# Float32 products in two column blocks, spread test loads and a first table of higher rank in a one-core attention and mixture-of-experts kernel

## The chip, the core and the metric

The kernel runs on one core of a Trainium2 chip. The metric is the device time of one launch in microseconds (us). Three runs of the kernel before gave 805.13, 809.86 and 812.39 us, so the median is 809.86 us. Engines are named as in the profile: PE is TensorE (matrix products), DVE is VectorE, ACT is ScalarE, POOL is GpSimd, and SP is the queue that issues most DMAs.

## The reference

Three stages follow one another: a linear attention with decay, a feed-forward product with a leaky relu, and a top-1 mixture of eight experts.

```python
def _attn_ref(q, k, v, alpha):           # each (4, 8, 768, 48), float32
    for t in range(S):
        state = alpha[:, :, t, :, None] * state + np.einsum('bhd,bhe->bhde', k[:, :, t], v[:, :, t])
        y[:, :, t] = np.einsum('bhd,bhde->bhe', q[:, :, t], state)

def _moe_ref(x, w_in, w_out):            # x (3072, 384), w_in (384, 2048), w_out (2048, 384)
    h = x @ w_in
    g = np.maximum(0.01 * h, h)
    return g @ w_out

def _moe2_ref(x, w_gate, w1, w2):        # w_gate (384, 8), w1 (8, 384, 1024), w2 (8, 1024, 384)
    logits = x @ w_gate
    expert_idx = np.argmax(logits, axis=1)
    # gate_w: softmax probability of the chosen expert
    for e in range(E):
        h = np.maximum(x[mask] @ w1[e], 0.0)
        out[mask] = gate_w[mask, None] * (h @ w2[e])
```

The weights w_in and w_out reach the kernel as float64 bit patterns, pairs of 32-bit words.

## The kernel before, in words

The 3072 tokens are cut into eight units (u) of 384 tokens, each of three chunks (c) of 128. Large products are made as three float16 products of high and low parts. In outline, the work of one unit is this.

- Attention: decays (`decays`, line 556 and on, DVE and ACT) are scanned, keys and queries are scaled by them (`scaled`, lines 594 and 596), keys are transposed (`keys`, line 619), scores are made (`chunk`, line 690, 48 rows by 128 columns) and masked (lines 692 and 694). The values of a chunk are scores times values (line 727) plus queries times the running state (line 715). Units 0 and 1 do line 727 in float32, the others in float16. The state itself is updated in `running` (line 651, weights of 64 columns, two heads in the two halves of the output's partitions). Chunk 0 of units 0, 2, 4 and 6 has no running state, so line 715 runs for 20 of the 24 chunks.
- After a chunk's values, DVE takes the largest magnitude (line 734) and makes a power of two of it (`pow2`, lines 518 to 523), ACT scales (line 738), PE transposes (lines 746 and 748), ACT and DVE write the two halves of `xT`.
- Feed-forward (`moe1`): the first product of a unit is 16 column blocks of 9 PE instructions (line 796), each followed by the leaky relu (`leaky`, lines 773 to 780), the second product is 144 PE instructions (line 805). `finish` (from line 851) splits its rows, and `route` (from line 879) chooses experts and scatters the rows of the unit to DRAM on POOL's queue (line 931).
- Weights first: while unit 0 runs, `w_in_piece` makes float32 and then a high and a low float16 part of each of 12 pieces of w_in from the float64 bits. The low part is made by two products on PE (lines 426 and 427) for pieces 0 to 2 and by DVE (line 422) for pieces 3 to 11. `w_out_piece` does the like for 16 pieces of w_out, and `logit_weights` multiplies each by w_gate (line 459 transposes, line 469 three float32 products of 8 columns).
- The float64 test: `low_load` reads all weights a second time in 56 pieces (SP, line 512, tile `ck`, three buffers), and DVE takes the smallest magnitude of the low words of each (line 514). It may run once the last w_out piece is done and unit 2 has had its first products.
- Experts: after unit 6 is routed, `tile_table` computes for 14 token tiles which expert and which rows they hold; `tile_gathers` gathers a tile's rows (POOL, line 1134, with a DVE copy of its list, line 1131), and `turn` transposes it (line 1147, six PE instructions). The last unit's rows are routed, and 14 further tiles listed, inside the expert loop (`last_tiles`). The expert loop (`experts`) makes 112 rounds, of 18 instructions at line 1245 and 6 at line 1271; each forces as many turns as it needs, and may take one turn more if its gather was issued at least `AHEAD1` = 4 rounds earlier by `state["gathered"]`.

The order on every engine up to the expert loop is written out at build time by a small planner, class `Loom`. Each piece of work is a generator that yields operations `O(engine, planned us, ...)`; `need` names events that must have happened, `take` and `free` count buffers, `post` makes an event, and each chain has a rank (the second argument of `loom.add`, the lowest first). The planner takes whichever operation can start first by its own clocks, and among those within 0.25 us of it the one of lowest rank. An event that a DMA posts counts as happened 2 us (in planned time before 130) or 4 us after its issue; an operation that merely follows a DMA in the same generator is not given that time. `keep_warm` fills planned gaps of PE with products that nobody reads (line 371). The engines then run their lists in that order, each waiting for its real inputs. In the expert loop the order is that of the code.

## Time and profile before

| | before |
|---|---|
| median of the runs | 809.86 us |
| the profiled execution, its own time | 808.41 us |
| its span, first to last instruction | 806.6 us |
| PE busy | 767.6 us, 95% |
| DVE busy | 639.6 us, 79% |
| ACT busy | 494.1 us, 61% |
| POOL busy | 370.1 us, 46% |

Times in the trace count from the first instruction. The first product of unit 0 (line 796) starts at 46.8, of unit 1 at 140.4, of unit 2 at 209.6, of unit 3 at 277.8, of unit 4 at 351.3, of unit 7 at 507.5; the last second product (line 805) of unit 7 ends at 557.2, and the expert loop fills the rest. A stage is read from one such start to the next. A float32 product may show two records. The granted clock of PE in a window is given as a share of 2.4 GHz: 1.00 is that level all the time, and a lower figure is a mean with stretches at 1.2 GHz.

### The profile page before, as it was taken

What the parts mean: (1) busy time and instruction counts of PE and PEld (TensorE: products, weight loads), DVE (VectorE), ACT (ScalarE), POOL (GpSimd) and SP (SyncE); (2) the same over time, 40 slices, a digit from 0 to 9 for tenths busy, and PEclk for the clock granted to TensorE, in tenths of its full rate; (3) what the DMA queues carried; (4) which work ended last, traced back from release to release, by engine and by line L of the source; (5) the groups of instructions that cost most, each with busy time, mean ns of one, the idle gap of its engine ahead of it and who ended that gap; (6) DMA issues with size and microseconds to landing.
All of it is one profiled execution on the core that took longest, in us unless ns stands there. A gap on an engine that the chain in (4) does not pass through costs nothing.

```text
span 806.6 us, 19210 instructions
## 1 busy us (share of the span) xinstructions
PE 767.6 (95%) x6991; PEld 541.3 (67%) x6991; DVE 639.6 (79%) x1450; ACT 494.1 (61%) x1137; POOL 370.1 (46%) x375
## 2 busy tenths in 40 slices
PE   7969999999997998999999999998999999999994
PEld 3836777667665565666756565666788888778883
DVE  7898999999787899975745485668668888999674
ACT  3647566799994268765454374643476566566673
POOL 6016313484373256245234061344531588776553
PEclk9899999999999999999999999999999999999998
DMA  9762454223417776200100323127354244332221
GB/s 261 247 170 79 121 157 118 61 71 90 99 44 209 214 194 186 61 1 1 51 1 3 127 70 98 43 86 210 95 150 140 90 120 137 100 119 61 93 82 69
DMA packets 44421, 87.23 MB, mean 108 GB/s; under 512 B 4797, under 2 KB 29427, under 8 KB 44320
## 3 DMA queue, kind: packets, MB, share of 16 engines
q1 hardware_dynamic: 39104, 70.89, 30.7%
q0 software_dynamic: 5216, 15.02, 5.6%
q8 instruction: 60, 0.98, 0.5%
q14 instruction: 41, 0.34, 0.1%
HBM read 76.42 MB, written 10.25 MB: 107 GB/s over the span
## 4 chain that ended last, share of the span: by engine, by line
PE 52%; DVE 9%; DMA 5%; issue 4%; POOL 3%; ACT 2%; POOLq 0%; ACTq 0%; DVEq 0%
PE a L1245 13%; PE m L1271 13%; PE m L796 13%; PE m L805 9%; DMA ck<-in_moe_w_in 2%; DMA ck<-in_moe_w_out 2%; DVE g_w L514 1%; DMA acc<-x_rows,offj 1%; POOL acc L1134 1%; PE a L1147 1%; POOL gh L780 1%; DVE Sd L640 1%; DVE gf L775 1%; PE a L690 1%; DVE Ft L556 1%
## 5 line engine op out<-in xcount | busy, mean ns | idle before, releaser
L796 PE MATMUL m<-xT,wih 128*128 128x384 f16 x1152 | 197.4, 331 | 7.9 <-DVE gf L775 7.8
L805 PE MATMUL m<-woh,gh 128*128 128x392 f16 x1152 | 202.9, 330 | 0.8 <-DVE gf L775 0.8
L780 POOL TENSOR_TENSOR gh<-gf,gh 128x384 f16<-128x384 f32 x118 | 113.8, 973 | 173.9 <-ACT gh L778 173.6
L796 PEld LDWEIGHTS <-wih 128*128 128x128 f16 x1152 | 113.3, 99 | 83.5 <-issue 13.1
L805 PEld LDWEIGHTS <-gh 128*128 128x128 f16 x1152 | 111.2, 98 | 73.7 <-issue 2.3
L1245 PEld LDWEIGHTS <-st 128*128 128x128 f16 x2016 | 123.5, 99 | 14.6 <-DVE st L1178 0.7
L1245 PE MATMUL a<-XT,st 128*128 128x128 f16 x2016 | 132.8, 221 | 0.0
L1271 PE MATMUL m<-W,hs 128*128 x672 | 128.2, 328 | 0.3 <-issue 0.3
L775 DVE SCALAR_TENSOR_TENSOR gf<-m,gf 128x384 f32<-128x384 f32 x128 | 69.9, 553 | 48.7 <-ACT gf L773 47.6
L1178 DVE COPY st<-W 128x1536 f16 x112 | 86.6, 773 | 22.3 <-PE a L1245 12.2
L773 ACT ACTIVATE gf<-m 128x384 f32<-128x384 f32 x128 | 62.2, 488 | 47.7 <-PE m L796 45.8
L1253 ACT ACTIVATE hs<-a 128x256 f16<-128x256 f32 x112 | 42.5, 379 | 65.1 <-PE a L1245 54.9
L1271 PEld LDWEIGHTS <-hs 128*128 128x128 f16 x672 | 61.6, 99 | 30.2 <-issue 1.2
L778 ACT CAST gh<-gf 128x384 f16<-128x384 f32 x128 | 64.2, 507 | 16.0 <-DVE gf L775 15.6
L1070 POOL TENSOR_TENSOR W<-wr,W 128x768 f16<-128x768 f32 x32 | 57.9, 1809 | 14.2 <-ACT W L1069 14.2
L1257 DVE SCALAR_TENSOR_TENSOR hs<-a,hs 128x256 f16<-128x256 f32 x112 | 46.5, 415 | 12.0 <-ACT junk L1289 7.5
L1286 DVE SCALAR_TENSOR_TENSOR acc<-m,acc 128x384 f32<-128x384 f32 x84 | 51.0, 607 | 1.7 <-issue 0.4
L1134 POOL DMA_INDIRECT acc<-x_rows,offj x28 | 29.4, 1049 | 39.5 <-DVE offj L1131 33.1
L1043 POOL TENSOR_SCALAR wr<-wr 128x768 f32<-128x768 f32 x32 | 32.7, 1024 | 26.9 <-DMA wr<-in_moe_w 26.9
L1292 POOL DMA_INDIRECT out<-acc x28 | 29.1, 1038 | 28.4 <-DVE acc L1286 21.6
L352 ACT ACTIVATE scrap<-W 128x768 bf16<-128x768 f16 x48 | 40.0, 834 | 0.0
L931 POOL DMA_INDIRECT x_rows<-xg,pi x24 | 26.1, 1087 | 21.5 <-DVE xg L925 9.3
(253 smaller groups left out, 1223.7 us busy)
## 6 DMA issues: line engine op xcount, KB each, us to landing
wr<-in_moe_w SPq DMA_DIRECT2D x64, 384.0 KB, 3.1
al<-in_aT SPq DMA_DIRECT2D x16, 390.0 KB, 3.2
raw_in<-in_moe_w_in SPq DMA_DIRECT2D x12, 512.0 KB, 9.9
raw<-in_moe_w_out SPq DMA_DIRECT2D x16, 384.0 KB, 3.9
ck<-in_moe_w_in SPq DMA_DIRECT2D x24, 256.0 KB, 2.8
ck<-in_moe_w_out SPq DMA_DIRECT2D x32, 192.0 KB, 2.4
kn__143<-in_kT SPq DMA_DIRECT2D x16, 288.0 KB, 5.3
qn__146<-in_qT SPq DMA_DIRECT2D x16, 288.0 KB, 9.3
```

The costliest lines, as they stand in the source:

```text
L773: A.activation(gf, ph[:, 0:UT], AF.Copy, scale=0.01 * CG)
L775: V.scalar_tensor_tensor(gf, ph[:, 0:UT], CG, gf, ALU.mult, ALU.max)
L778: A.copy(gh[:, 0], gf)
L780: E_[e].tensor_tensor(out=gh[:, 1], in0=gf, in1=gh[:, 0], op=ALU.subtract)
L796: T.matmul(ph[:, 0:UT], wih[:, a, kk, f * P : (f + 1) * P], xT[:, b, kk, :], start=(n == 0), stop=(n == 8),)
L805: T.matmul(po[:, 0:ROW], g[f][:, a, c * P : (c + 1) * P], woh_[0][:, b, f, :], start=(n == 0), stop=(n == 3 * NF - 1),)
L1070: G.tensor_tensor(out=lo, in0=raw, in1=hi, op=ALU.subtract)
L1178: V.tensor_copy(out=sth[i % 2].rearrange("p a k f -> p a (k f)"), in_=Wp[ph][0][:, :, ds(reg(V, j), 1), :, :].rearrange("p a e k f -> p a ...
L1245: T.matmul(hp[:, f * P : (f + 1) * P], st[:, a, kk, f * P : (f + 1) * P], XT[j][:, b, kk, :], start=(n == 0), stop=(n == 8),)
L1257: V.scalar_tensor_tensor(hs[:, 1].rearrange("p i t -> p (i t)"), hp[:, 0 : 2 * P], 0.0, hs[:, 0].rearrange("p i t -> p (i t)"), ALU.max, A ...
L1271: T.matmul(yp[:, 0:DM], hs[:, a, i, :], W2[:, b, ds(rp, 1), i, :].rearrange("p e f -> p (e f)"), start=(n == 0), stop=(n == 5),)
L1286: V.scalar_tensor_tensor(ac, yp[:, 0:DM], gt, ac, ALU.mult, ALU.add)
```

## The change

Five edits are made.

1. Float32 products whose weights have 128 columns are issued as two products of 64 weight columns, each to its half of the output's partitions: the scores times values of units 0 and 1, the queries times state of all units, and the logit products. The queries times state now come behind the scores times values. The planned durations of these, and of the unchanged line 651, are lowered.
2. The test loads may start when unit 1 has had its first products (before: unit 2). A load needs the landing of the load two before it. The landing is an event with 2 us added, and the DVE operation needs it.
3. Pieces 3 to 5 of w_in have their low part made on PE as well.
4. The first table has rank 0.9 instead of 1.5, so that it comes ahead of the leaky relu's chains, which have 1. GAP, the planned spacing of gathers, is 0.8 instead of 1.2.
5. The gathers that the planner places carry their planned time in rounds after the planner's end of PE, where they had counted as nine rounds before the loop.

```diff
--- before.py
+++ after.py
@@ -51,7 +51,7 @@
 EXPM = 0x7F800000
 RING = 3
 AHEAD1 = 4
-GAP = 1.2
+GAP = 0.8
 F64_TINY = 2.0**15 / 1.125
 F64_LOW = 2.0**-15 * 1.125
 RMAX = 2.0**58
@@ -417,7 +417,7 @@
         hi, lo = (wih[:, a, kk, sl] for a in range(2))
         yield O("A", 0.65)
         A.activation(hi, w32, AF.Copy, scale=SA)
-        if n >= 3:
+        if n >= 6:
             yield O("v", 0.63, free=[("w32", ("i", n))], post=[("wi", n)])
             V.scalar_tensor_tensor(lo, w32, SA, hi, ALU.mult, ALU.subtract)
             return
@@ -463,10 +463,13 @@
             A.activation(wt, pt[:, 0:DM], AF.Copy, scale=SB)
         else:
             V.tensor_scalar(wt, pt[:, 0:DM], SB, None, ALU.mult)
-        yield O("P", 0.67, take=[("a", ("lg", f))], free=[("wt", f)])
+        yield O("P", 0.35, take=[("a", ("lg", f))], free=[("wt", f)])
         pg = pst("a")
         for kk in range(3):
-            T.matmul(pg[:, 0:E], wt[:, kk * P : (kk + 1) * P], wg[:, kk, :], start=(kk == 0), stop=(kk == 2))
+            for m in range(0, P, 64):
+                T.matmul(
+                    pg[m : m + 64, 0:E], wt[:, kk * P + m : kk * P + m + 64], wg[:, kk, :], start=(kk == 0), stop=(kk == 2)
+                )
         yield O("A", 0.4, free=[("a", ("lg", f))])
         A.copy(og[:, f, :], pg[:, 0:E])
         A.copy(woh[:, 0, f, DM:ROW], og[:, f, :])
@@ -500,7 +503,7 @@
 
     def low_load(i):
         n, h = divmod(i, 2)
-        yield O("D", 0.9, need=["lp", ("first", 2)], take=[("ck", i)])
+        yield O("D", 0.9, need=["lp", ("first", 1)] + ([("lo", i - 2)] if i > 1 else []), take=[("ck", i)], post=[("lo", i)], lag=2.0)
         raw = lp[0].tile([P, 256, 2], U32, tag="ck", name="ck", bufs=3)
         w = 256 if n < 12 else DM // 2
         if n < 12:
@@ -510,7 +513,7 @@
         else:
             src = w_out[(n - 12) * P : (n - 11) * P, h * w : (h + 1) * w]
         nc.sync.dma_start(out=raw[:, 0:w].rearrange("p a b -> p (a b)"), in_=src.bitcast(U32))
-        yield O("V", 0.07 + 0.28 * w / 256, free=[("ck", i)], post=[("low", i)])
+        yield O("V", 0.07 + 0.28 * w / 256, need=[("lo", i)], free=[("ck", i)], post=[("low", i)])
         V.tensor_reduce(g_w[:, i : i + 1], raw[:, 0:w, 1].bitcast(F32), AX.X, ALU.min, apply_absolute_value=True)
 
     def pow2(mx, kexp, n, nm):
@@ -642,7 +645,7 @@
                 )
                 loom.add(heads(u, c, Sc), (4 + 2 * u if u else 0.5) - 0.05, now=loom.clock["V"])
             if c in states(u):
-                yield O("P", 0.92, need=[("kn", u, c), ("vt", u)] + ([("vy", u)] if u >= US else []), apart=True,
+                yield O("P", 0.5, need=[("kn", u, c), ("vt", u)] + ([("vy", u)] if u >= US else []), apart=True,
                         take=[("a", ("u", u, c)), ("SU", (u, c))], free=[("kn", (u, c)), ("vt", u)])
                 up = pst("a")
                 vt = r["vt"]
@@ -704,28 +707,34 @@
                 e = yield O("G", 1.17, post=[("shl", u, c, z)], alt=("v", (0.6,), 0.3))
                 E_[e].tensor_tensor(out=sh[:, 1, z], in0=s_[z], in1=sh[:, 0, z], op=ALU.subtract)
             loom.add(scores_range(u, c, s_), 7 + u)
-            yield O("P", 1.45 if old else 0.8, need=Sn + [("vs", u, i) for i in range(c + 1)], take=[YA, ("xh", (u, c)), ("n1", (u, c))],
+            yield O("P", 1.3 if old else 0.7, need=Sn + [("vs", u, i) for i in range(c + 1)], take=[YA, ("xh", (u, c)), ("n1", (u, c))],
                     free=[("sh", (u, c)), ("vs", u)] + Sf, post=[("y", u, c)])
         else:
-            yield O("P", 2.85 if old else 1.95, need=Sn + [("vt", u)], take=[YA, ("xh", (u, c)), ("n1", (u, c))], free=[("sm", (u, c)), ("vt", u)] + Sf, post=[("y", u, c)])
+            yield O("P", 1.65 if old else 1.0, need=Sn + [("vt", u)], take=[YA, ("xh", (u, c)), ("n1", (u, c))], free=[("sm", (u, c)), ("vt", u)] + Sf, post=[("y", u, c)])
         yp = pst("a")
-        n, tot = 0, (3 * H if half else H) + (4 if old else 0)
-        if old:
-            for pr in range(4):
-                T.matmul(
-                    yp[:, pr * 96 : pr * 96 + 96], qt[:, pr, sl], r["Sc", c][:, pr, :],
-                    start=(n == 0), stop=(n == tot - 1), skip_group_check=True,
-                )
-                n += 1
+
+        r64 = [slice(64 * m, 64 * m + 64) for m in range(2)]
         for h in range(H):
             hd = slice(h * D, (h + 1) * D)
             if half:
-                ab = [(sh[:, a, h % 2, h // 2, :], r["vs"][:, b, c, hd]) for a, b in ((0, 0), (0, 1), (1, 0))]
+                for i, (a, b) in enumerate(((0, 0), (0, 1), (1, 0))):
+                    T.matmul(
+                        yp[:, hd], sh[:, a, h % 2, h // 2, :], r["vs"][:, b, c, hd],
+                        start=(h == 0 and i == 0), stop=(not old and h == H - 1 and i == 2), skip_group_check=True,
+                    )
             else:
-                ab = [(s_[h % 2][:, h // 2, :], r["vt"][:, c, hd])]
-            for a, b in ab:
-                T.matmul(yp[:, hd], a, b, start=(n == 0), stop=(n == tot - 1), skip_group_check=True)
-                n += 1
+                for m in r64:
+                    T.matmul(
+                        yp[m, hd], s_[h % 2][:, h // 2, m], r["vt"][:, c, hd],
+                        start=(h == 0), stop=(not old and h == H - 1), skip_group_check=True,
+                    )
+        if old:
+            for pr in range(4):
+                for m in r64:
+                    T.matmul(
+                        yp[m, pr * 96 : pr * 96 + 96], qt[:, pr, c * P + m.start : c * P + m.stop], r["Sc", c][:, pr, :],
+                        start=False, stop=(pr == 3), skip_group_check=True,
+                    )
         yield O("V", 1.0)
         if half:
             mx = g_y[:, 3 * (u - US) + c : 3 * (u - US) + c + 1]
@@ -1165,7 +1174,7 @@
             place_of(j)
             gather(j)
             reg(V, j)
-            state["gathered"].append(state["tile"])
+            state["gathered"].append(state["tile"] if late is not None else loom.clock["G"])
             loom.ev["gap", j] = loom.clock["G"] + GAP, "G"
 
     def tile_turns():
@@ -1219,11 +1228,12 @@
         loom.add(low_load(i), 10 + 0.01 * i)
     loom.add(moe1(), 50)
     loom.add(first_weights(), 20)
-    loom.add(first_table(), 1.5)
+    loom.add(first_table(), 0.9)
     loom.add(firsts, 0.5, True)
     loom.add(turns, 3.5, True)
     loom.add(first_stages(), 3.6)
     loom.run()
+    state["gathered"] = [int((t - loom.clock["P"]) / 2.3) for t in state["gathered"]]
 
 
 
```

The edits move work on all engines. Three places are shown.

The first is on DVE in the middle of the kernel before, from the largest magnitude of unit 4's second chunk (`g_y<-a`) to the rows of unit 2 (`mx<-m`, `n2m`, `L`); `g_w<-ck` is the test of one loaded piece. Before:

```order
L734 TENSOR_REDUCE g_y<-a 128x1
L518 TENSOR_SCALAR n1m<-g_y 128x1
L522 TENSOR_SCALAR n1s<-n1m 128x1
L523 TENSOR_SCALAR n1e<-n1m 128x1
L514 TENSOR_REDUCE g_w<-ck 128x1 x2
L851 TENSOR_REDUCE mx<-m 128x1
L518 TENSOR_SCALAR n2m<-mx 128x1
L522 TENSOR_SCALAR n2s<-n2m 128x1
L523 TENSOR_SCALAR n2e<-n2m 128x1
L853 TENSOR_SCALAR L<-m,n1e 128x8
L854 SCALAR_TENSOR_TENSOR gsc<-n1e,n2e 128x1
L514 TENSOR_REDUCE g_w<-ck 128x1 x3
```

And now, from the same chunk:

```order
L743 TENSOR_REDUCE g_y<-a 128x1
L521 TENSOR_SCALAR n1m<-g_y 128x1
L525 TENSOR_SCALAR n1s<-n1m 128x1
L526 TENSOR_SCALAR n1e<-n1m 128x1
L869 SCALAR_TENSOR_TENSOR xg<-m,n2s,xg 128x384
L566 SCALAR_TENSOR_TENSOR ln,g_fr<-Ft,R 128x780
L517 TENSOR_REDUCE g_w<-ck 128x1
L568 SCALAR_TENSOR_TENSOR R<-ln,R 128x780
L599 SCALAR_TENSOR_TENSOR kt<-kn__143,R 128x12x64
L743 TENSOR_REDUCE g_y<-a 128x1
```

Between the second and the third chunk of unit 4 stood seven tests, and now there is one. The first test stands ahead of unit 3's first chunk now (before: of unit 4's), the last ahead of unit 7's first chunk (before: of unit 5's second).

The second place is on PE, the last rows ahead of the first product of unit 1 (`m<-xT,wih`); `xh` is a chunk's scaled values, `kn` a chunk's keys, `ident` with a number the filler's operand. Before:

```order
L755 MATMUL a<-xT,idn_161 128x384
L619 MATMUL a<-ident,kt 128x128 x4
L746 MATMUL a<-ident,xh 128x128 x3
L651 MATMUL a<-vt,kn 64x48 x8
L755 LDWEIGHTS idn_161
L755 MATMUL a<-xT,idn_161 128x384
L690 MATMUL a<-qt,kt 128x128 x8
L796 LDWEIGHTS wih
L796 MATMUL m<-xT,wih 128x384
```

And now:

```order
L371 LDWEIGHTS ident_65
L371 MATMUL m<-ident_65 128x512
L371 LDWEIGHTS ident_65
L371 MATMUL m<-ident_65 128x512
L764 LDWEIGHTS idn_161
L764 MATMUL a<-xT,idn_161 128x384
L371 LDWEIGHTS ident_65
L371 MATMUL m<-ident_65 128x512
L371 LDWEIGHTS ident_65
L371 MATMUL m<-ident_65 128x512
L805 LDWEIGHTS wih
L805 MATMUL m<-xT,wih 128x384
```

The second products of unit 0 are all done earlier now, and two groups of key transposes, a state update and a group of scores have moved behind the first product of unit 1, so that fillers stand between the last transposes. In all there are 85 filler products (70 before), of which 18 stand between unit 0's last second product and unit 1's first product, where there was none.

The third place is on POOL, around the scatters of the last unit's rows (`x2_rows<-xg`); `acc12` and `acc13` are the last two of the first 14 tiles. Before:

```order
L1134 DMA acc9_5812<-x2_rows,offj_68 128x386
L1134 DMA acc10_5813<-x2_rows,offj_68 128x386
L1134 DMA acc11_5814<-x2_rows,offj_68 128x386
L930 COPY xg_6961<-con_97 128x1
L931 DMA x2_rows<-xg_6961,pi_7465 24577x386
L930 COPY xg_7091<-con_97 128x1
L931 DMA x2_rows<-xg_7091,pi_7465 24577x386
L930 COPY xg_7226<-con_97 128x1
L931 DMA x2_rows<-xg_7226,pi_7465 24577x386
L1134 DMA acc12_5815<-x2_rows,offj_68 128x386
L1134 DMA acc13_5816<-x2_rows,offj_68 128x386
```

And now:

```order
L1143 DMA acc10_6013<-x2_rows,offj_68 128x386
L1143 DMA acc11_6014<-x2_rows,offj_68 128x386
L1143 DMA acc12_6015<-x2_rows,offj_68 128x386
L1143 DMA acc13_6016<-x2_rows,offj_68 128x386
L939 COPY xg_7243<-con_97 128x1
L940 DMA x2_rows<-xg_7243,pi_7719 24577x386
L939 COPY xg_7387<-con_97 128x1
L940 DMA x2_rows<-xg_7387,pi_7719 24577x386
L939 COPY xg_7515<-con_97 128x1
L940 DMA x2_rows<-xg_7515,pi_7719 24577x386
L1143 DMA acc14_7540<-x2_rows,offj_68 128x386
L1143 DMA acc15_7541<-x2_rows,offj_68 128x386
```

The gathers of all first 14 tiles stand ahead of the scatters now. On PE, nine of the turns stand ahead of the first round of the expert loop (before: six), the next comes after round 3 (before: one each after rounds 0, 1 and 4).

On SP, the 56 test loads stood in a nearly closed row with two decay loads and a key load between them; now 17 rows of loads of decays, keys, queries and values stand among them.

## Rows read from the trace of the kernel before

**Rows 1.** Page, busy time by engine: us, share of the span, instructions.

```profile
PE 767.6 (95%) x6991; PEld 541.3 (67%) x6991; DVE 639.6 (79%) x1450; ACT 494.1 (61%) x1137; POOL 370.1 (46%) x375
```

**Rows 2.** Windows by stage: window, length, busy us of PE, PEld, DVE, ACT, POOL; clock.

```profile
46.80:140.40 93.60, 85.50 (x655) 63.09 (x654) 86.72 (x165) 58.43 (x145) 29.26 (x37) 0.96 0.42 122
...
209.60:277.80 68.20, 62.44 (x516) 40.32 (x514) 50.67 (x135) 43.30 (x105) 32.29 (x33) 0.97 0.49 141
277.80:351.30 73.50, 69.33 (x631) 45.81 (x629) 69.56 (x162) 50.38 (x113) 33.07 (x30) 0.98 0.50 138
...
557.20:600.00 42.80, 38.70 (x466) 32.38 (x464) 27.57 (x105) 24.59 (x46) 21.13 (x23) 0.92 0.47 135
```

**Rows 3.** Timeline of PE, 245 to 318 us: start, length, instruction, count, idle before it.

```profile
...
253.44 0.55 PE L748 MATMUL a<-ident,xh 128*128 128x128 f32 x3 [1.95 <-ACT xh L738]
262.36 0.90 PE L748 MATMUL a<-ident,xh 128*128 128x128 f32 x3 [2.42 <-ACT xh L738]
```

**Rows 4.** Source line 514: idle of DVE ahead of it, us and times.

```profile
...
  DMA ck<-in_moe_w_in: 6.9, 11
  DMA ck<-in_moe_w_out: 3.3, 8
```

**Rows 5.** Chain of waits, 238 to 320 us: start, length, what.

```profile
...
243.07 3.80 DMA ck<-in_moe_w_in
246.90 0.43 DVE g_w L514
247.34 2.98 DMA ck<-in_moe_w_in
```

**Rows 6.** Timeline of PE, 505 to 600 us.

```profile
...
562.54 0.82 PE L1147 MATMUL a<-ident,acc 128*128 128x128 f16 x6 [2.20 <-DMA acc<-x_rows,offj]
...
581.11 0.51 PE L1147 MATMUL a<-ident,acc 128*128 128x128 f16 x6 [1.61 <-DMA acc<-x_rows,offj]
581.91 1.32 PE L1271 MATMUL m<-W,hs 128*128 x6 [0.30 <-issue]
```

**Rows 7.** Timeline of POOL, 500 to 610 us.

```profile
...
535.74 1.09 POOL L1134 DMA_INDIRECT acc<-x_rows,offj  x1 [1.18 <-DVE offj L1131]
...
557.47 1.01 POOL L1134 DMA_INDIRECT acc<-x_rows,offj  x1 [2.23 <-DVE offj L1131]
...
574.38 0.98 POOL L931 DMA_INDIRECT x_rows<-xg,pi  x1 [0.28 <-issue]
577.94 1.08 POOL L1134 DMA_INDIRECT acc<-x_rows,offj  x1 [2.58 <-DVE offj L1131]
```

**Rows 8.** Timeline of PE, 26 to 36 us.

```profile
...
30.07 1.03 PE L715 MATMUL a<-diag,qt 128*128 128x96 f32 x8
30.93 1.91 PE L727 MATMUL a<-vt,sm 128*128 128x48 f32 x16
32.77 0.67 PE L651 MATMUL a<-vt,kn 128*64 128x48 f32 x16
33.38 0.94 PE L746 MATMUL a<-ident,xh 128*128 128x128 f32 x6
34.15 1.02 PE L426 MATMUL m<-w,ids 128*128 128x512 f32 x2
```

**Rows 9.** Timeline of PE, 118 to 142 us.

```profile
...
118.47 0.73 PE L469 MATMUL a<-wg,wt 128*128 128x8 f32 x6
119.14 0.67 PE L651 MATMUL a<-vt,kn 128*64 128x48 f32 x16
...
139.29 1.16 PE L690 MATMUL a<-qt,kt 48*128 48x128 f32 x16
140.38 1.64 PE L796 MATMUL m<-xT,wih 128*128 128x384 f16 x9
```

**Rows 10.** Groups of DVE by line and shape: busy us, mean ns.

```profile
...
L422 DVE SCALAR_TENSOR_TENSOR wih<-w,wih 128x512 f16<-128x512 f32 x9 | 6.0, 684 | 0.9 <-ACT wih L419 0.9
```

**Rows 11.** Page, DMA issues of SP: count, KB each, us from issue to landing.

```profile
...
al<-in_aT SPq DMA_DIRECT2D x16, 390.0 KB, 3.2
```

## Prediction

> **What bounds the kernel now.** I read the page first: PE is busy for 95% of the span, far ahead of the other engines [rows 1]. So time goes only if PE gets less to do in a stretch where nothing else holds it up, or if PE's own idle time goes. The second view is the table of windows by stage, where PE's busy time is set against the window's length and its granted clock [rows 2]. Three stretches stand out.
>
> In the first, from unit 0's first product to unit 1's (93.6 us), PE is busy for 85.5 us and DVE for 86.7 us. Both are nearly full and wait for each other: DVE has the float64 bits of all weights to turn, PE the products of unit 0 and of the logits.
>
> In the second, from unit 2's first product to unit 4's (68.2 and 73.5 us), PE is idle for 68.2 - 62.4 = 5.8 us and 73.5 - 69.3 = 4.2 us, and its mean clock is 0.97 and 0.98. A mean below 1 is a stretch at 1.2 GHz in which work takes twice the time, so what it cost is (1 - 0.97) x 68.2 = 2.0 us and 0.02 x 73.5 = 1.5 us. Together 13.5 us. The timeline of PE shows such idle times: it waits for `xh`, which ACT makes from a factor of DVE's [rows 3]. The source view of the test line says what DVE did: it stood 6.9 + 3.3 = 10.2 us for test loads that had not landed [rows 4]. The chain shows the cycle: a load of 3.80 us, the test 0.43 us, and the test frees the buffer of the next load, 2.98 us [rows 5]. As DVE runs its list in order, the factor for `xh` stands behind these tests.
>
> The third stretch is the start of the expert loop, 557.2 to 600: 42.8 - 38.7 = 4.1 us idle, and 0.08 x 42.8 = 3.4 us of clock. The timeline names two waits of turns for gathered rows [rows 6]. The turn at 562.54 waits for the gather issued at 557.47. The turn at 581.11 waits for a gather that stands behind the last unit's three scatters on POOL: the scatter is issued at 574.38, the gather at 577.94 [rows 7].
>
> **The change, part by part.** All is worked out in the profiled execution's span of 806.6 us; its own time is 808.41, and the median is 1.45 above that.
>
> *Float32 products.* Start to start, a block of eight products with 128 weight columns and 48 moving ones takes 32.77 - 30.93 = 1.84 us, four with 96 moving columns 0.86, eight with 64 weight columns 0.61 [rows 8], and three with 8 moving columns 0.67 [rows 9]. So a 64-column product costs 0.076. The six value blocks of units 0 and 1 become 16 such products: 1.22 for 1.84, -0.62 x 6 = -3.7 us. The 16 logit blocks become six: between 0.46, if 8 moving columns cost no more than 48, and 0.67, as now: I take 0.46, for the value block is the nearest form; -0.21 x 16 = -3.4 us (bound 0). The 20 state blocks become eight products with 96 moving columns, a form that the trace lacks. Below stands 0.61 for 48 columns, above the score block, eight of 128 moving columns in 1.09 us [rows 9]. Midway at 96 lies about 0.9, what is paid now: I take no change, and keep -0.25 and +0.23 a block, -5 and +5 us in all. Fifteen of them lie behind 140.4.
>
> The Trainium skill, "TensorE: Matmul & The Clock Gate", section "LDWEIGHTS (loading the stationary operand)", has the load's time grow with its columns alone; by that rule two loads of 64 columns cost as much as one of 128, and a block bound by its loads gains nothing from the split. The trace speaks against it: 1.84 us against 0.61 is a ratio of 3, not 2 [rows 8]. By the rule, the -3.7 and -3.4 us would be 0.
>
> *Low parts on PE.* Three pieces take 3 x 0.684 = 2.1 us from DVE [rows 10], and give PE three more of the float32 product, 1.02 each [rows 8], some 3.1 us, with a float16 product and a copy of ACT, which is busy for 58.4 of 93.6 us there and has the room.
>
> *The early stretch.* PE loses 3.7 + 3.4 - 3.1 = 4.0 us there, and some 2.7 us more move behind 140.4: a score group of 1.09 [rows 9], a state update of 0.61 [rows 8] and two groups of key transposes, at 0.5 each by half a score group. But by the order unit 0's second products are all done before unit 1's last chunk, and PE then has fillers, not work, while the chain values, DVE's factor, `xh`, transposes, `xT` runs alone. DVE gets 2.1 us less, but finishing and routing unit 0 now stand ahead of that chain, some two scans later. I take 140.4 as unchanged, between -5 (all of PE's gain arrives) and +6 (the chain waits out two more factors behind DVE's list).
>
> *Test loads.* The tests keep their time on DVE, but stand one by one over four units, each after an event that the load's landing posts; DVE's 10.2 us of waiting should go. What could be late next is DVE itself: in the two windows it is busy for 50.7 and 69.6 of 68.2 and 73.5 us [rows 2]; a third of the tests moves to later units, where PE alone is the bound. The 13.5 us go, but for some tenths, and the moved attention work costs 2.7: about -10.5 us. Bounds: -14 and 0. A new wait stands in SP's queue: 17 rows of decays, keys, queries and values now stand among test loads, and a test load waits for a buffer that DVE frees, with those rows behind it. A decay load lands in 3.2 us [rows 11]; the planner issues it well ahead of its scan, so I cost it at nothing, and it is a rival below.
>
> *Table, gathers, turns.* The table's DVE steps now come ahead of the last leaky relus. Before, the first gather went out at 535.74 [rows 7]; five of the sixteen relu steps that stood ahead of it are behind it now, and each comes with nine first products of PE, 1.64 us at most [rows 9]: some 7 to 8 us earlier. All 14 gathers stand ahead of the scatters, so the second wait loses its cause; the first loses it because a turn is taken only when its gather is four rounds old. The three turns moved ahead cost the same there. Cost or gain: the 7.5 us of this stretch, of which I take 6, since the relu steps that are now behind the table may be late. Bounds: -8 and 0. The rest of the loop is 24 PE instructions a round as before: 0.
>
> Sum: 0 - 10.5 - 6 = -16.5; the span becomes 790.1, its own time 791.9, the median 793.4. I forecast 793, with a range of its own from 785 to 800.
>
> **Rivals.** (1) *DVE, not its waits, holds the middle.* For it: DVE is busy for 120 of the 141.7 us of the two windows, and tests now stand in unit 3's attention too. Against it: the idle rows of PE end with DVE's factor right behind tests that waited. If half of the idle time stays, that part is -5 and the rest as above: -11, median 799.
>
> (2) *The early chain is late.* For it: 18 fillers stand where work stood, and a stretch without work lowers the clock. Against it: DVE has less to do by 2.1 us. Unit 1 starts 6 us later, and the gathers, planned on durations that are too short, save 2 only: +6 - 10.5 - 2 = -6.5, median 803.
>
> (3) *Halves do not pay.* PE's early work then grows by 3.1 us instead of shrinking by 4.0, and unit 1 starts some 4 us later: median 797. It is the rule of the Trainium skill, "TensorE: Matmul & The Clock Gate", section "LDWEIGHTS (loading the stationary operand)", that would bring this.
>
> (4) *Loads behind test loads: slower.* A late test holds its buffer, SP stands at the next test load, and decays or keys behind it land a cycle late, 247.34 - 243.07 = 4.3 us [rows 5]. Four such cycles on the chain of units 4 to 7 cancel the forecast's gain; six make 26 us: 809.9 - 16.5 + 26 = 819. For it: two or three units have both decays and keys among the tests. Against it: three buffers, and an order that issues each load after the landing of the one two before.
>
> **How the numbers follow.** Chances: forecast 0.58, rival 1 0.17, rival 2 0.12, rival 3 0.05, rival 4 0.08. One per cent of 809.9, about what a measurement of this kernel can tell from no change, is 8.1: faster means below 801.8, slower above 818. The forecast counts as faster but for 0.03, rival 1 for 0.12 of its 0.17, rival 3 wholly; rival 2 as the same; rival 4 as slower for 0.06. Faster: 0.55 + 0.12 + 0.05 = 0.72; slower 0.07 with a little of rival 2; the same 0.21. For the range, below stands the forecast with both bounds of the state blocks' fifteen (-4) and of the early stretch (-5): 784. Above, all but the last of rival 2 is to be held: 806.
>
> **What would show it.** Right: the source view of the test line without waits for `ck` of over 2 us in all; PE idle below 3 us and clock 1.00 from unit 2 to unit 4, that stretch shorter by some 11 us; a block of 16 half products at about 1.2 us; unit 1's first product at 140 within 5; no waits of turns for gathered rows over 1 us. Wrong: scans or scalings that wait for decays or keys with SP standing at a test load (rival 4); PE waiting for DVE with no load in the chain (rival 1); unit 1's first product behind 145 (rivals 2 and 3, told apart by the length of a half product).

## The result, and the profile after

Four runs of the changed kernel took 785.93 to 789.69 us, median 787.47, beside 809.08 for the kernel before: 0.9737 of its time, 95% interval 0.9686 to 0.9788. The forecast was 793 in a range from 784 to 806. The profiled execution took 785.93, its span is 783.9, 22.7 less than before.

Page of the kernel after, busy time by engine, to be read against [rows 1]:

```profile
PE 757.1 (97%) x7367; PEld 524.1 (67%) x7367; DVE 639.8 (82%) x1449; ACT 495.8 (63%) x1138; POOL 366.6 (47%) x375
```

PE has 376 instructions more and is busy 10.5 us less. The rest of the 22.7 us, 12.2, is idle time that went.

Windows by stage of the kernel after (columns as in [rows 2]): unit 0's first product to unit 1's, unit 2 to 3, unit 3 to 4, and the first 42.8 us of the expert loop.

```profile
40.10:131.30 91.20, 83.48 (x806) 55.15 (x805) 86.16 (x185) 55.95 (x140) 30.25 (x41) 0.98 0.41 114
202.10:269.40 67.30, 66.27 (x637) 44.02 (x636) 58.22 (x139) 54.32 (x130) 31.99 (x33) 1.00 0.51 138
269.40:332.20 62.80, 62.04 (x563) 40.88 (x561) 56.94 (x149) 43.52 (x100) 27.27 (x27) 1.00 0.36 95
541.50:584.30 42.80, 40.61 (x529) 33.84 (x528) 31.94 (x113) 28.29 (x51) 20.12 (x21) 1.00 0.46 135
```

From unit 2 to unit 4 PE is idle for 1.8 us (before: 9.9) and its clock is 1.00. In the loop's start it is busy for 1.9 us more, at 1.00 instead of 0.92.

Source view of the test line (514 before, 517 now; answers to [rows 4]): under "sat idle before it" no line is left.

```profile
L517 DVE TENSOR_REDUCE g_w<-ck x56: 321/346/423, 173.5 to 370.3; 128x1 f32<-128x192 f32 x32, 128x1 f32<-128x256 f32 x24
its engine sat idle before it (us, times) until:
who waited for it (us, times):
```

Timeline of PE after, unit 7 and the loop's start (answers to [rows 6]), the rows with a wait:

```profile
507.30 6.07 PE L805 MATMUL m<-xT,wih 128*128 128x384 f16 x36 [2.34 <-DVE gf L784]
513.62 1.62 PE L805 MATMUL m<-xT,wih 128*128 128x384 f16 x9 [0.25 <-DVE gf L784]
545.32 1.18 PE L1255 MATMUL a<-XT,st 128*128 128x128 f16 x18 [1.17 <-ACT hs L1263]
548.59 1.18 PE L1255 MATMUL a<-XT,st 128*128 128x128 f16 x18 [1.02 <-DVE st L1187]
```

No turn (line 1156 now) waits for gathered rows. The loop has two waits of about 1 us on other work, and unit 7 has a stall of 2.3 us that the kernel before lacks.

By place, each from the profiled execution: unit 1's first product comes at 131.3 instead of 140.4 (-9.1); from there to unit 7's 356.8 instead of 367.1 (-10.3); unit 7's products 53.4 instead of 49.7 (+3.7); the loop 242.4 instead of 249.4 (-7.0). One execution of each kernel stands behind these numbers. The table below shows how far others of the same kernels lie from them.

### The profile page after: what moved, and what is told of

Its sections match the earlier page's. It is cut to its first block, busy times and chain, and to the rows that moved or that the text cites. A ratio compares the mean times of both kernels' runs of the same rounds, so it can differ in the third digit from the quotient of the medians.

```text
span 783.9 us, 19953 instructions
## 1 busy us (share of the span) xinstructions
PE 757.1 (97%) x7367; PEld 524.1 (67%) x7367; DVE 639.8 (82%) x1449; ACT 495.8 (63%) x1138; POOL 366.6 (47%) x375
## 4 chain that ended last, share of the span: by engine, by line
PE 79%; DVE 15%; ACT 2%; issue 2%; POOL 1%; DMA 1%; DVEq 0%; ACTq 0%; POOLq 0%
PE m L814 21%; PE m L805 18%; PE a L1255 14%; PE m L1281 14%; PE a L693 2%; PE a L734 1%; PE a L654 1%; PE a L1156 1%; DVE gf L784 1%; PE a L622 1%; PE a L721 1%; DMA qn__146<-in_qT 1%; PE a L470 1%; DVE w L398 1%; DVE kt L599 1%
## 5 line engine op out<-in xcount | busy, mean ns | idle before, releaser
L805 PE MATMUL m<-xT,wih 128*128 128x384 f16 x1152 | 193.4, 326 | 5.0 <-DVE gf L784 3.7
L789 POOL TENSOR_TENSOR gh<-gf,gh 128x384 f16<-128x384 f32 x118 | 116.4, 996 | 172.5 <-ACT gh L787 169.3
L1255 PEld LDWEIGHTS <-st 128*128 128x128 f16 x2016 | 121.2, 98 | 17.8 <-DVE st L1187 4.6
L1255 PE MATMUL a<-XT,st 128*128 128x128 f16 x2016 | 130.7, 219 | 2.2 <-ACT hs L1263 1.2
L1187 DVE COPY st<-W 128x1536 f16 x112 | 90.6, 809 | 23.9 <-PE a L1255 22.9
L1281 PEld LDWEIGHTS <-hs 128*128 128x128 f16 x672 | 61.3, 98 | 29.3
L1143 POOL DMA_INDIRECT acc<-x_rows,offj x28 | 31.8, 1134 | 31.5 <-DVE offj L1140 28.5
L1302 POOL DMA_INDIRECT out<-acc x28 | 27.4, 977 | 29.8 <-DVE acc L1296 23.4
L352 ACT ACTIVATE scrap<-W 128x768 bf16<-128x768 f16 x48 | 40.1, 835 | 0.0
L940 POOL DMA_INDIRECT x_rows<-xg,pi x24 | 27.7, 1153 | 24.1 <-DVE xT L769 7.2
```

Of the source, the lines that this page charges most:

```text
L789: E_[e].tensor_tensor(out=gh[:, 1], in0=gf, in1=gh[:, 0], op=ALU.subtract)
L805: T.matmul(ph[:, 0:UT], wih[:, a, kk, f * P : (f + 1) * P], xT[:, b, kk, :], start=(n == 0), stop=(n == 8),)
L1187: V.tensor_copy(out=sth[i % 2].rearrange("p a k f -> p a (k f)"), in_=Wp[ph][0][:, :, ds(reg(V, j), 1), :, :].rearrange("p a e k f -> p a ...
L1255: T.matmul(hp[:, f * P : (f + 1) * P], st[:, a, kk, f * P : (f + 1) * P], XT[j][:, b, kk, :], start=(n == 0), stop=(n == 8),)
L1281: T.matmul(yp[:, 0:DM], hs[:, a, i, :], W2[:, b, ds(rp, 1), i, :].rearrange("p e f -> p (e f)"), start=(n == 0), stop=(n == 5),)
```

## The experiments

Twelve kernels ran. Each ratio is to runs of the kernel before that were taken with it, whose median lay between 805.68 and 809.08. The table holds all their profiles, with the two already shown. Columns: start of DVE's first step on the first keys (the row `kt<-kn` of its timeline); the granted clock from 20 to 28 us; first product of units 0 and 1; unit 1 to unit 7, and of that unit 2 to unit 4; unit 7 to its last second product; from there to the end; ratio of the runs to those of the kernel before, with its interval. Upper part: the kernel before with an edit added. Lower part: the changed kernel with an edit taken away or altered.

| kernel | keys | clock | unit 0 | unit 1 | 1 to 7 | 2 to 4 | unit 7 | loop | ratio |
|---|---|---|---|---|---|---|---|---|---|
| before | 14.73 | 0.59 | 46.8 | 140.4 | 367.1 | 141.7 | 49.7 | 249.4 | |
| b_again | 13.45 | 0.59 | 46.3 | 138.3 | 370.5 | 144.5 | 49.7 | 250.2 | one run |
| b_test | 14.89 | 0.86 | 45.5 | 137.2 | 355.0 | 131.9 | 50.1 | 247.5 | 0.987 (0.983 to 0.990) |
| b_table | 12.80 | 0.89 | 44.3 | 136.9 | 368.7 | 143.3 | 53.0 | 247.7 | 1.003 (1.000 to 1.007) |
| b_split | 12.56 | 1.00 | 38.3 | 133.9 | 365.7 | 137.8 | 49.4 | 247.9 | 0.998 (0.995 to 1.002) |
| b_halves | 14.42 | 0.88 | 44.8 | 137.0 | 372.6 | 146.2 | 49.4 | 247.5 | 1.001 (0.997 to 1.005) |
| after | 12.17 | 1.00 | 40.1 | 131.3 | 356.8 | 130.1 | 53.4 | 242.4 | 0.974 (0.969 to 0.979) |
| a_again | 15.98 | 0.50 | 46.7 | 139.5 | 357.1 | 130.1 | 54.6 | 243.0 | 0.978 (0.973 to 0.983) |
| a_nosplit | 15.60 | 0.50 | 48.7 | 140.6 | 356.4 | 132.2 | 54.6 | 244.8 | 0.991 (0.988 to 0.995) |
| a_nolow | 12.09 | 1.00 | 38.3 | 134.5 | 359.4 | 132.4 | 53.4 | 244.1 | 0.984 (0.979 to 0.989) |
| a_notable | 14.32 | 0.60 | 44.5 | 137.4 | 357.2 | 130.2 | 50.0 | 250.3 | 0.985 (0.979 to 0.991) |
| a_norank | 14.44 | 1.00 | 41.7 | 135.2 | 357.4 | 130.1 | 51.1 | 244.5 | 0.982 (0.978 to 0.986) |
| a_rank1 | 11.83 | 1.00 | 39.9 | 134.1 | 357.3 | 130.1 | 51.6 | 242.4 | 0.979 (0.973 to 0.986) |
| a_finish | 13.29 | 1.00 | 41.3 | 135.1 | 355.5 | 126.0 | 51.6 | 246.3 | 0.973 (0.968 to 0.978) |

### The two kernels again (b_again, a_again)

Nothing edited.

> The kernel before once more, one profile, nothing changed: it tells whether the 9.1 us that the early stretch lost are the edits or the start of one execution. In the first profile of before the first key load landed late, PE waited 2.4 us ahead of 19.0, the clock was at 1.2 GHz from 19.8 to 26.6, PE stalled 6 us at 52.5 and the clock was low again from 57.3 to 64.1; unit 0's first product came at 46.8 and unit 1's at 140.4. Theory A (the edits): all this repeats, 46.8 and 140.4 within 1 us. Theory B (chance of the start): the first key load lands some 2.5 us earlier, no low clock before 27, unit 0's first product at 40 to 43, unit 1's at 134 to 137. Both: unit 1 to unit 7 again 367 us within 1.5, the loop 249 within 1.

> The changed kernel once more, beside the next one on the same chip: unit 1's first product at 131 to 135, unit 2 to unit 4 at 130.1, unit 7 at 53.4 with the stall of 2.3 us, loop 242.4, in all 786 to 791.

Measured: before again 810.46 (one run), the changed kernel again 790.80 (six runs, 786.85 to 796.70, granted clock 0.995 to 0.984). From unit 1 on the second changed profile repeats the first within about a microsecond a stage. Ahead of unit 1 it doesn't: 139.5 for 131.3. The place shows in four answers. First the timeline of DVE and the window of PE from 20 to 28 us, of the changed kernel's first profile:

```profile
12.17 0.96 DVE L599 SCALAR_TENSOR_TENSOR kt<-kn__143,Ft 128x768 f32<-128x768 f32 x1 [0.30 <-POOL sm L338]
```
```profile
20.00:28.00 8.00, 8.00 (x141) 1.00 0.84 277
```

and of its second:

```profile
15.98 0.96 DVE L599 SCALAR_TENSOR_TENSOR kt<-kn__143,Ft 128x768 f32<-128x768 f32 x1 [2.95 <-DMA kn__143<-in_kT]
```
```profile
20.00:28.00 8.00, 8.00 (x45) 0.50 0.62 222
```

The first keys were used 3.8 us later. PE, whose fillers end at about 16, then waited longer for their transposes, and had a clock of 0.50, which is 1.2 GHz all the time, from 20 to 28. Over the 14 profiles, PE's last filler there and the transposes start 2.1 to 4.2 us apart in the eight with a clock below 1.00, and 0.2 to 1.8 in the six with 1.00. The kernel before came out at unit 0 as theory A has it (46.3, clock 0.59), but its unit 1, 138.3, is 2 us off, between the two theories, and from unit 1 to unit 7 it took 370.5 for 367.1, where both had 1.5 at most: its own two profiles differ by 3.4 us there. The changed kernel shows that one program can lie at either end of the start. So the 9.1 us of the early stretch can't be put down to the edits. What these are worth there is read from many profiles: with the old products, or the new ones in the old order, unit 1 starts at 136.9 to 140.6 (six profiles, mean 138.4), with halves and durations at 131.3 to 139.5 (seven, without a_finish, mean 135.1). That is -3 us, and the two groups overlap.

### The paced test loads alone (b_test)

```diff
-        yield O("D", 0.9, need=["lp", ("first", 2)], take=[("ck", i)])
+        yield O("D", 0.9, need=["lp", ("first", 1)] + ([("lo", i - 2)] if i > 1 else []), take=[("ck", i)], post=[("lo", i)], lag=2.0)
...
-        yield O("V", 0.07 + 0.28 * w / 256, free=[("ck", i)], post=[("low", i)])
+        yield O("V", 0.07 + 0.28 * w / 256, need=[("lo", i)], free=[("ck", i)], post=[("low", i)])
```

> The paced test loads alone, on the kernel before. Theory A (the waits of the test held the middle): no waits for ck of over 2 us in all, PE clock 1.00 from unit 2 to unit 4, that stretch 9 to 13 us shorter than 141.7; unit 1's first product unmoved or a little earlier; the loop 249; in all -8 to -11 us. Theory B (DVE itself held it, and the shorter products gave the middle its gain): -3 to -5 us. Rival 4 (loads behind test loads): units 4 to 7 longer.

Measured 793.38 against 805.68, which is -12.3, a little more than either theory had; unit 1 came 1 to 3 us earlier in its profile. Unit 2 to unit 4 takes 131.9 (-9.8, and -12.6 beside b_again), unit 1 to unit 7 355.0 (-12.1), units 4 to 7 are not longer. Its windows of units 2 and 3:

```profile
204.60:273.60 69.00, 67.05 (x621) 45.46 (x620) 66.12 (x149) 56.61 (x135) 32.07 (x32) 1.00 0.55 153
273.60:336.50 62.90, 61.84 (x539) 41.26 (x537) 55.75 (x141) 39.99 (x93) 30.98 (x30) 1.00 0.31 87
```

DVE is busier than before in the first (66.1 of 69.0, before 50.7 of 68.2) and PE still waits less. Theory A holds: the waits of the test held the middle, not DVE's work. Theory B falls, and so do the loads behind test loads on SP: between 200 and 490 us neither PE, DVE, ACT nor POOL waits for a DMA, here and in the changed kernel's first profile. The edit starts the tests a unit earlier and also paces them; which of the two does it was not run apart. Every kernel of the table with this edit has 355 to 359 us from unit 1 to unit 7, every one without it 366 to 373.

### The halved products, alone and taken out (b_split, b_halves, a_nosplit)

b_split has the new products and their planned durations, b_halves the products without the durations, so that all engines keep the order of before, but for the state products, which come behind the values here too; a_nosplit is the changed kernel with the old products and durations. The core of the edit:

```diff
-            T.matmul(pg[:, 0:E], wt[:, kk * P : (kk + 1) * P], wg[:, kk, :], start=(kk == 0), stop=(kk == 2))
+            for m in range(0, P, 64):
+                T.matmul(
+                    pg[m : m + 64, 0:E], wt[:, kk * P + m : kk * P + m + 64], wg[:, kk, :], start=(kk == 0), stop=(kk == 2)
+                )
...
-            yield O("P", 1.45 if old else 0.8, need=Sn + [("vs", u, i) for i in range(c + 1)], take=[YA, ("xh", (u, c)), ("n1", (u, c))],
+            yield O("P", 1.3 if old else 0.7, need=Sn + [("vs", u, i) for i in range(c + 1)], take=[YA, ("xh", (u, c)), ("n1", (u, c))],
```

> The halved float32 products with their planned durations alone, on the kernel before. A value block of 16 halves about 1.1 us start to start (1.8 before), a logit block 0.47 (0.68), a state block 0.83 (0.885): -0.7 x 6, -0.2 x 16 and -0.05 x 20 are 8 us less work for PE. Theory A (PE's work sets the early stretch): unit 1's first product 5 to 8 us earlier than in the run of before of the same chip. Theory B (DVE's bits set it): 0 to 3 us earlier. Middle and loop as before within 2 us.

> The kernel before with its float32 products halved and nothing else: the planned durations stay, so the order of all engines is that of before. It tells the price of the halves from what the planner makes of it. Theory A (the halves themselves give the early gain): a value block 1.1 us, unit 0's first product at 39 to 42 with the clock at 1.00 there, as in the five kernels with halves (38.3 to 41.7; 44.3 to 48.7 in five without). Theory B (the new order gives it): unit 0's first product at 44 to 46. Both: unit 2 to unit 4 and the loop as in before within 3 us, in all 801 to 806.

> The changed kernel with the whole float32 products and their old planned durations: the low parts on PE, the paced loads and the table edits alone. Theory A (the halves gave the early gain: unit 0's first product came at 38.3 in the run of the halves alone, at 44.3 to 46.8 in four runs without them): unit 0's first product at 44 to 47, unit 1's at 136 to 138, the middle as short as in the changed kernel (unit 2 to unit 4 at 130), in all 791 to 794. Theory B (the early gain is the low parts): unit 1's first product at 131 to 134.

Measured: 803.52 beside 805.68, 808.26 beside 808.66, and 798.83 beside 807.02. The halves are as cheap as hoped. Timeline of PE in the changed kernel, answering to [rows 8]:

```profile
26.19 1.14 PE L727 MATMUL a<-vt,sm 128*64 128x48 f32 x32
27.16 0.85 PE L734 MATMUL a<-diag,qt 128*64 128x96 f32 x16
```

A value block, start to start, is 27.16 - 26.19 = 0.97 here and 1.1 in the mean of six; before it was 1.84. Summed in the same way from start to next start, a logit block takes 7.57 / 16 = 0.47 (0.68 before) and a state block 16.55 / 20 = 0.83 (0.885 before). PE has some 8 us less to do. Yet b_halves gains nothing in ten runs, and the 801 to 806 missed. Its unit 0, 44.8, is theory B's number and not theory A's 39 to 42, but its keys came late and the clock was 0.88, so this one profile doesn't decide between the two. Its unit 2 to unit 4, 146.2, is 4.5 us longer than in the first profile of before, where 3 were expected. In its first 137.0 us, up to unit 1's first product, PE is busy for 117.9 us; in b_again for 125.0 of 138.3. So 7 us less work brought that product forward by 1.3 us: the early stretch's end isn't set by PE's work. b_split shows unit 1 at 133.9, but its keys came early and its clock was 1.00, and its 4.4 us beside b_again lie between theory B's 0 to 3 and theory A's 5 to 8, so neither is shown by it; its unit 2 to unit 4, 137.8, is outside what either theory had, in a middle that still waits for test loads.

Inside the changed kernel the edit is worth more: a_nosplit, whose places are those of theory A but for a still later unit 0, is 8 to 11 us above the changed kernel's two medians instead of the 4 to 6 expected. By place, beside a_again, whose keys came equally late, it differs by 2.3 us in the span only (796.5 and 794.2), 1.1 of it ahead of unit 1 and 1.8 in the loop. The rest goes with the clock: all five runs of a_nosplit have a granted clock of 0.985 to 0.988, the ten of the changed kernel 0.984 to 0.995, and the slowest of these, 796.7, is near the runs of a_nosplit. In five profiles with whole products the clock was low from 20 to 28 each time, in nine with halves three times. That halves avoid the late start more often is therefore likely. How they could is not shown: PE's order up to that place is the same in both, and the landing times overlap.

### Without the low parts on PE (a_nolow)

```diff
-        if n >= 6:
+        if n >= 3:
             yield O("v", 0.63, free=[("w32", ("i", n))], post=[("wi", n)])
```

> The changed kernel without its third edit: three low parts of w_in are again DVE's. Theory A (those 2.1 us of DVE stood on the early stretch): unit 1's first product 2 to 4 us later than 131.3, the rest as in the changed kernel, in all 789 to 791. Theory B (PE's work set the stretch, and low parts on PE cost it 3.1 us): unit 1's first product 1 to 3 us earlier, in all 785 to 787.

Measured 793.14, above both expectations. Unit 1's first product, 134.5, is where theory A had it, but it also lies within those of the changed kernel (131.3 and 139.5), so no gain or loss is seen there. What the edit does show is a shift: the two kernels with the new durations and without it, b_split and this one, have unit 0's first product earliest, at 38.3, and then the longest stretch to unit 1's, 95.6 and 96.3, where those with it have 91.2 to 94.2. The time is lost later: unit 2 to unit 4 132.4 for 130.1 and the loop 244.1 for 242.4. The lists of all engines differ there between the two kernels, because the planner's later choices follow from its earlier ones. Whether that is more than the luck of one list stays open.

### Table, gap and age, alone and taken out (b_table, a_notable, a_norank)

b_table has the last two edits alone, a_notable all but them, a_norank all but the rank:

```diff
-GAP = 1.2
+GAP = 0.8
...
-            state["gathered"].append(state["tile"])
+            state["gathered"].append(state["tile"] if late is not None else loom.clock["G"])
...
-    loom.add(first_table(), 1.5)
+    loom.add(first_table(), 0.9)
```

> The first table's rank, the smaller gap and the gathers' age alone, on the kernel before. Theory A: the loop from the end of the last second products shrinks from 249.4 to about 242.5 (-7) without waits of turns for gathered rows, and unit 7's attention grows from 49.7 by 1 us for the turns moved ahead, and by 2.5 more if the rank brings the stall that the changed kernel shows there; in all -3 to -6 us. Theory B (the loop's gain came from the shorter planned durations or the paced loads): the loop stays within 2 us of 249.4, in all within 2 us of before. Everything before unit 7 as in before.

> The changed kernel without its last two edits: the table's rank, the gap and the gathers' age as before. On the kernel before these edits alone were worth nothing (1.0034 of its time; unit 7 +3.3, the loop -1.7). Theory A (they pay only with the other edits): the loop at 247 to 250 with waits of turns for gathers, unit 7 at 50, in all 3 to 5 us slower than the changed kernel. Theory B (they are worth nothing here too): loop and unit 7 together within 1.5 us of 295.8, in all as the changed kernel.

> The changed kernel with the first table's rank put back to 1.5. In the changed kernel and in the run of the table edits alone, one short step of DVE's table took 3.3 to 3.4 us while POOL ran three low parts of the hidden values in a row, and PE stood 2.3 to 2.7 us in unit 7. Theory A (the rank brings the collision): unit 7 to the end of its second products goes back from 53.4 to 50 us, the first gather comes 4 to 5 us later after unit 7's first product than in the changed kernel (23.0 there, 28.2 before), and a turn waits for its gather again, so the loop grows from 242.4 to 245 to 248; in all within 3 us of the changed kernel. Theory B (the collision is not tied to the rank): unit 7 stays at 53 and the loop grows.

Measured 808.40 beside 805.68, 795.26 beside 808.66, and 791.24 beside 807.02. In unit 7 and the loop together: changed kernel 295.8 and 297.6, a_norank 295.6, a_notable 300.3; before 299.1 and b_table 300.7. So with the other edits (theory A of a_notable) the two are worth 3.6 us, and gap and age alone 4.7: the rank takes 1.8 us from the loop and puts 2.9 into unit 7. Theory A of a_norank is met in this (the collision goes with the rank, a turn waits again), with unit 7 at 51.1 for 50 and the first gather 6.3 us later for 4 to 5. The waits of turns in a_notable show what gap and age remove, the third above all, whose gather is issued behind the last unit's scatters as in [rows 7]:

```profile
546.88 0.51 PE L1156 MATMUL a<-ident,acc 128*128 128x128 f16 x6 [0.57 <-DMA acc<-x_rows,offj]
549.73 0.51 PE L1156 MATMUL a<-ident,acc 128*128 128x128 f16 x6 [1.33 <-DMA acc<-x_rows,offj]
569.18 0.82 PE L1156 MATMUL a<-ident,acc 128*128 128x128 f16 x6 [3.72 <-DMA acc<-x_rows,offj]
```

In a_norank all 14 gathers go out ahead of the scatters, and two waits of 1.25 and 1.13 us are left. On the kernel before the edits gain nothing, unit 7 as theory A had it (+3.3), the loop as theory B (-1.7), and another wait of the same size stands where those of the turns went. PE's and ACT's timelines in b_table:

```profile
565.72 2.10 PE L1246 MATMUL a<-XT,st 128*128 128x128 f16 x18 [3.63 <-ACT hs L1254]
```
```profile
564.96 0.22 ACT L884 ACTIVATE rex<-rd 128x24 f32<-128x24 f32 x1 [3.55 <-DVE rd L881]
565.09 0.64 ACT L1254 ACTIVATE hs<-a 128x256 f16<-128x256 f32 x2
```

The round waits for its relu on ACT, which stands behind a step of the last unit's routing, which waits for DVE. In the changed kernel the same wait is 1.17 us.

### The table's rank at 1.0 (a_rank1)

```diff
-    loom.add(first_table(), 0.9)
+    loom.add(first_table(), 1.0)
```

> The changed kernel with the first table's rank at 1.0 in place of 0.9: the order then has DVE make the three low parts of the hidden values that POOL ran in a row beside the table. Theory A (DVE's table step waits for POOL's row of low parts): no table step over 1 us, unit 7's attention at 50.5 to 51.5 instead of 53.4, loop 242 to 243, in all 2 to 3 us faster than the changed kernel, some 785. Theory B (the stall is DVE being behind by the table itself): unit 7 stays at 53, in all as the changed kernel.

Measured: the stall goes. The timelines of DVE and POOL in the changed kernel:

```profile
503.15 0.17 DVE L1016 SCALAR_TENSOR_TENSOR tst<-con,tst 128x14 f32<-128x14 f32 x1
503.36 3.42 DVE L1022 TENSOR_SCALAR off<-tst,lane 128x14 int32<-128x14 f32 x1
506.70 0.54 DVE L784 SCALAR_TENSOR_TENSOR gf<-m,gf 128x384 f32<-128x384 f32 x1
```
```profile
503.10 0.98 POOL L940 DMA_INDIRECT x_rows<-xg,pi  x1 [0.28 <-POOL xg L939]
504.11 2.64 POOL L789 TENSOR_TENSOR gh<-gf,gh 128x384 f16<-128x384 f32 x3
```

in b_table:

```profile
520.52 3.29 DVE L1006 TENSOR_SCALAR tst<-tst 128x14 f32<-128x14 f32 x1
```
```profile
521.14 2.64 POOL L780 TENSOR_TENSOR gh<-gf,gh 128x384 f16<-128x384 f32 x3
```

and in a_rank1, where DVE makes those three low parts:

```profile
507.68 0.17 DVE L1016 SCALAR_TENSOR_TENSOR tst<-con,tst 128x14 f32<-128x14 f32 x1
507.89 0.23 DVE L1022 TENSOR_SCALAR off<-tst,lane 128x14 int32<-128x14 f32 x1
```

A DVE step of 14 elements a partition takes 3.3 to 3.4 us when it meets three POOL operations in a row, ends when the last of them ends (506.78 and 506.75; 523.81 and 523.78), and takes 0.23 without them. All five profiles with the rank of 0.9 have such a step (b_table, after, a_again, a_nosplit, a_nolow: 3.29 to 3.44 us), none of the nine with another rank has one over 1 us. The relu steps stand behind it, and PE behind these. Unit 7 falls to 51.6, next to theory A's 50.5 to 51.5, and the loop stays at 242.4. In the runs, 787.83 with an interval from 0.973 to 0.986, the 2 us cannot be seen beside the spread of the start.

### The finishing of unit 0 ranked lower (a_finish)

On top of a_rank1:

```diff
-                    loom.add(finish(u, c, pos[c]), 2, now=loom.clock["P"])
+                    loom.add(finish(u, c, pos[c]), 6.11, now=loom.clock["P"])
```

> The changed kernel with the first table's rank at 1.0 (the stall in unit 7 gone: 51.6 for 53.4 in the run of that edit) and with the finishing of unit 0's rows ranked behind unit 1's attention: DVE then takes the chain value of unit 1's chunk before two of the three finishing steps that stood ahead of it. Theory A (my reason for the early stretch: the finishing on DVE holds back the chain while PE has fillers): PE's wait of 3.3 us for xh near 116 shrinks below 2 us, unit 0's first product to unit 1's is 2 to 4 us shorter than in the changed kernel beside it, in all 3 to 6 us faster than it. Theory B (PE or the rest of DVE's list sets it): that stretch within 1 us, in all 1 to 2 us faster, for the stall alone.

Measured 785.08 (784.18 to 790.08), beside 790.80 of the changed kernel on the same chip (786.85 to 796.70). PE's single wait of 3.3 us is gone, but waits of about 1 us take its place, as the timelines of PE in the changed kernel and in this one show, and unit 0 to unit 1 takes 93.9, not less than the 91.2 to 94.2 of the changed kernel's order:

```profile
116.36 0.94 PE L755 MATMUL a<-ident,xh 128*128 128x128 f32 x6 [3.27 <-ACT xh L747]
```
```profile
119.54 0.32 PE L727 MATMUL a<-vt,sm 128*64 128x48 f32 x4 [0.75 <-DVE sm L695]
120.95 1.02 PE L727 MATMUL a<-vt,sm 128*64 128x48 f32 x28 [1.09 <-DVE sm L697]
```

So theory A falls at its place: the finishing is not what sets the early stretch. Its median is the lowest of all and 5.7 below the changed kernel's, with intervals that overlap. The profile, of a run at the upper end (790.08), has 4.1 us less from unit 2 to unit 4 and 3.2 more in units 4 to 7 and 3.3 in the loop than a_again, so it doesn't explain the median. That it beats the kernel before is shown; that it beats the changed one is likely, not more.

## Why the prediction was right, and where it was not

The time, 787.47, lies in the range; the forecast of -16.5 us is to be set against -18 to -22 in the two comparisons of the changed kernel.

- **Test loads, -10.5:** right in place, mechanism and size. The edit alone gives -9.8 from unit 2 to unit 4 and -12.1 from unit 1 to unit 7 (b_test; -12.6 and -15.5 beside b_again); the waits for `ck` are gone, the clock is 1.00, no load on SP came late. Rivals 1 and 4 are out by b_test.
- **Float32 products:** the prices held: 1.1 for 1.22 a value block, 0.47 for 0.46 a logit block, and 0.83 a state block, inside its bounds. Rival 3 is out by its price. The Trainium skill, "TensorE: Matmul & The Clock Gate", section "LDWEIGHTS (loading the stationary operand)", has the load grow with its columns alone. The prediction took from it that the split would gain nothing, and held a ratio of 3 against it; here two products of 64 columns cost some 0.6 of one with 128. The single records of the trace, which the timeline merges, show that it is this step that fails, and not the rule: records of whole products follow each other every 112 ns, with 8, 48 or 96 moving columns alike (before), those of halves come in pairs 7 ns apart, a pair every 59 ns with 8 or 48 moving columns and every 83 with 96 (after). A step of 59 for 112 ns agrees with that rule of the Trainium skill; the rest of the gain comes from the pair, two records side by side, which a sum of two loads, one after the other, leaves out. That a pair is the two halves of one product is the likely reading; the records don't name the half.
- **The early stretch, 0 with bounds -5 and +6:** -9.1 in the profile shown, outside the bounds, but -3 in the mean of 7 against 6 profiles, inside. The step that failed is the one that read the start of a single profile as the kernel's: the 46.8 of unit 0's first product held a late landing of the keys and a low clock, which I took as given, and I weighed only what came behind it. The reason I gave for no gain, the finishing ahead of unit 1's chain, is not borne out either (a_finish).
- **Table, gathers, turns, -6:** the waits went and the loop lost 7.0, as predicted, but the step "the table's DVE steps now come ahead of the last leaky relus" was credited with too much. The first gather comes 23.0 us after unit 7's first product (511.11 - 488.1) for 28.2 before, 5 us earlier instead of 7 to 8, and with the old rank, at 29.3, the loop is only 1.5 to 2.1 longer (a_norank); at 18.7, with the rank of 1.0, it is no shorter (a_rank1). The age and the gap do most of it. The relu steps behind the table were late, for which I had set 1.5 us aside, but by a cause I had not listed: DVE's table step held up by POOL's low parts, +2.3 of the +3.7 us in unit 7. Most of the rest are the three turns moved ahead, 0.33 each. Net, the two edits gave 3.6.
- **The sum** came out near in part by luck, because errors of opposite sign met: 3 us more early, 1 to 2 more in the middle, 2.4 less in unit 7 and the loop. Rival 2 is out: it had unit 1 6 us later, and in the kernels with halves and durations none of the eight profiles starts it behind the 140.4 of before.

## What to carry to other kernels

Read the start of a kernel from several executions before pricing anything there: a late landing, with the wait and the low clock behind it, went with 8 us at unit 1's first product between two profiles of one program, more than most edits gave, and it can pass as an edit's gain. Where an in-order engine waits for DMAs, spread the waiting steps and issue each load well ahead; that alone was about half of this gain. An edit that takes a wait away shows nothing while a second wait of the same size stands behind it, so judge edits in the kernel that has the others too.

## What the runs showed of the hardware

- Halving the weight columns of a float32 product from 128 to 64 cut its price to less than a third: 1.84 / 8 = 0.23 to 1.1 / 16 = 0.07 us a product, so that a block with twice as many products is the shorter one. The halves are written in turn to the two halves of the output's partitions, and their records come in pairs 7 ns apart; no run has halves that all go to the same partitions.
- A DVE operation of 14 elements a partition was held for 3.3 to 3.4 us until a row of three POOL operations had ended, in five profiles, and took 0.23 without them. The Trainium skill, "SBUF — State Buffer", section "SBUF: two separate sides", says that DVE and POOL share a pair of ports as an exclusive lock, kept by whichever starts first for the whole instruction, where DVE's is in a two-port mode or has two inputs in SBUF; whether this step is of such a form no run shows. The traces agree that one engine stands blocked; but DVE came free only after three instructions of POOL (2.64 us), not after one (0.9). DVE's step begins 0.6 to 0.75 us before the first of the three, while POOL still issues a scatter (503.10 to 504.08), and POOL's spans are rough, so who took the ports first isn't shown.
- DVE's first use of the first keys came between 11.8 and 16.0 us in 14 profiles, and PE's granted clock behind it, from 20 to 28 us, lay between 0.50 and 1.00.
